# Pooling attention and a four-expert layer: two tiles of the start done alike, with halves and another order

## The chip, the cores and the metric

The kernel runs on one core of one Trainium2 chip. The metric is the time of one execution on the device in microseconds (us), lower being better. A core has five engines that run side by side and wait for one another through semaphores: TensorE multiplies matrices (PE in the profile, and PEld for the loading of its stationary operand), VectorE (DVE) and ScalarE (ACT) work element by element, GpSimd (POOL) here issues nearly all loads, and SyncE (SP) issues the stores and some transposing transfers.

## The reference, cut to what matters

The input is attention with 8 batches, 8 heads, 576 tokens and head size 64. Keys and values are averaged over groups of 8 tokens, so each head has 72 keys. The result goes through four experts whose outputs are added, each weighted by a probability of the token.

```python
k_p = k.reshape(B, H, 72, 8, D).mean(axis=3)          # v_p likewise
scores = scale * q @ k_p.T                            # [576, 72] per head
attn = exp(scores - max(scores)); attn /= attn.sum() + 1e-9
x = (attn @ v_p) as [4608 tokens, 512]
p = domain_probs / (domain_probs.sum(-1) + 1e-9)
out = sum over e of p[:, e] * (relu(x @ w1[e]) @ w2[e])   # w1: 512x1024, w2: 1024x512
```

## The kernel before, in words

A tile is 128 tokens with all 8 heads. There are 36 tiles, and four of them make a group of 512 tokens. A *step* is one group with one expert, and there are 36 steps. In each step `up` (L453) makes the hidden values of 512 tokens, 32 products of 512 columns, and ScalarE applies the relu (L457). `down` (L486) makes the output of one tile, 8 products of 512 columns, and VectorE adds it, weighted, in `collect` (L497, L501). A steady loop at the end of the kernel goes through the steps. While it computes one step's `down` it computes the next step's `up`, and a plan by slots puts the attention of later tiles between them. It starts with `up` of step 1.

Ahead of that loop stands the *head*: the attention of the first four tiles, step 0's `up` for each of them alone (`up_tile`, L469, 32 products of 128 columns), and step 0's `down` of tiles 0 to 2. The head is written out by hand in the order in which each engine is to run it. The kernel has a manual schedule: every engine runs its instructions in the order in which they are written, and a wait holds up everything behind it on that engine.

The attention of a tile goes through these functions, which the change and the prediction name:

- `split_q` and `turn_q` (L310, L314): queries to bf16, turned on TensorE, and copied out of PSUM by ScalarE as `qT`.
- `scores` (L320): products with the keys, into the one PSUM buffer `sc`. The next tile's scores wait until VectorE has read it.
- `maxima` (L334) and `less` (L338), together `less_max`: the greatest score of each head, and the difference from it, on VectorE.
- `expo`: the exponential on ScalarE. For a tile that is "in rows" (`in_rows`) it writes bf16 `attn` undivided (L351). For the others it writes f32 `e_sb` (L358).
- `normalise` (L372 to L380): four VectorE instructions, the sum by head, the small constant, the reciprocal and the division, which writes bf16 `attn`.
- `attn_T` (L394, L395): five transposes on TensorE, and a copy out of PSUM as `attnT`.
- `context` (L436, L442): eight products which give x already turned, and a ScalarE copy to `xT`, the input of `up_tile`.
- `context_rows` (L410, L416), used for tile 0 and for the tiles from the third group on: five products that give x in rows, one token to a partition. VectorE divides by the sum while it copies to `x_sb`.
- For tile 0 alone, `sums0` (L636 to L643) gets the sums by five small products with the 0/1 mask `own`, and `turn_x0` (L648, L649) turns `x_sb` by four transposes and one ScalarE copy.

The values of batch 0 are summed by eight products (`sum_values0`, L615) and spread into `vbd` by two VectorE instructions that multiply by the mask `mask_v` (`spread_values0`, L624). `make_mask_v` (L185) writes that mask from `own`, which GpSimd makes early. `idle_products` (L572) are products of a zeroed tile whose result nobody reads. They stand where TensorE would wait.

PSUM buffers come from pools. `ps_t` (tag "t") and `ps_h` (tag "h") have two buffers each, which alternate, `ps_o` has two, and `ps_s` has one. GpSimd's queue issues the loads in a fixed order: keys and values of batch 0, `w1` of expert 0 in two halves, `w2` of expert 0, `w1` of expert 1, and so on. From the ninth load on each issue waits until the load eight places before it has landed.

Of the kernel before, what the change touches and what calls it, by code (L numbers as in the profile page):

```python
# [10 lines left out]
ALU = mybir.AluOpType  # L11
AX = mybir.AxisListType
BF16 = mybir.dt.bfloat16
F32 = mybir.dt.float32
# [3 lines left out]
def kernel(  # L18
# [10 lines left out]
    nc = tc.nc  # L29

    B, H, S, D = q.shape
    E, DM, F = moe_w1.shape
    P = nc.NUM_PARTITIONS
# [3 lines left out]
    KC = DM // P  # L37
    FB = F // P
    NTOK = B * S
    G = 512  # L40
    NG = NTOK // G
    TPG = G // P
# [7 lines left out]
    V_MEAN = 1.0 / POOL  # L50
# [133 lines left out]
    def make_mask_v():  # L184
        nc.vector.tensor_copy(  # L185
            out=mask_v[:].rearrange("p a z y d -> p (a z y) d"),
            in_=own[:].rearrange("p a z y -> p (a z y)").unsqueeze(2).to_broadcast(
                [P, NPAIR * 4, D]
            ),
        )  # L190
# [97 lines left out]
    attnT = {}  # L288
    xT = {}
# [4 lines left out]
    def by_dma(t):  # L294
        return t >= 2 * TPG


    def in_rows(t):
        return t == 0 or by_dma(t)

    def turn_q(t):
        qT[t] = qtp.tile([P, NPAIR, P], BF16, name="qT")
# [40 lines left out]
    def less_max(t):  # L343
        maxima(t)
        less(t)
# [55 lines left out]

    def context_rows(t):
        ps = ps_t.tile([P, DM], F32, tag="t", name="x_ps")
        for b, _, n, at in segments(t * P, P):
            flat = vbd[b][:].rearrange("p a z y d -> p (a z y d)")
            for i in range(NB):
                c0, c1, h0 = chunk(i)
                nc.tensor.matmul(  # L410
                    ps[at:at + n, h0 * D:(h0 + c1 - c0) * D],
                    lhsT=attnT[t][:, i, at:at + n], rhs=flat[:, c0 * D:c1 * D],
                    start=(i == 0), stop=(i == NB - 1), skip_group_check=True,
                )
        x_sb = soft.tile([P, DM], BF16, name="x_sb")
        nc.vector.scalar_tensor_tensor(  # L416
            out=x_sb[:].rearrange("p (h d) -> p h d", d=D),
            in0=ps[:].rearrange("p (h d) -> p h d", d=D), scalar=V_MEAN,
            in1=rss[t][:].unsqueeze(2).to_broadcast([P, H, D]),
            op0=ALU.mult, op1=ALU.mult,  # L420
        )
        return x_sb

    def context(t):
        g, col = t // TPG, (t % TPG) * P
        if t % TPG == 0:
            xT[g] = grp.tile([P, KC, G], BF16, name="xT")
        if by_dma(t):
            x_sb = x_sbs[t] = context_rows(t)
# [12 lines left out]
        nc.scalar.copy(out=xT[g][:, :, col:col + P], in_=ps[:])  # L442
# [14 lines left out]
        nc.scalar.activation(out=hs[s][:, fb, :], in_=ps[:], func=ACT.Relu)  # L457


    def up_tile(s, i):  # L460
        g, e = divmod(s, E)
        if i == 0:
            hs[s] = hpool.tile([P, FB, G], BF16, name="h_sb")
        cols = slice(i * P, (i + 1) * P)
        for f0 in range(0, FB, TPG):
            ps = ps_h.tile([P, TPG, P], F32, tag="h", name="h_ps")
            for f in range(TPG):
                for kc in range(KC):
                    nc.tensor.matmul(  # L469
                        ps[:, f], lhsT=w1_sb[e][:, kc, (f0 + f) * P:(f0 + f + 1) * P],  # L470
                        rhs=xT[g][:, kc, cols], start=(kc == 0), stop=(kc == KC - 1),
                    )
# [92 lines left out]
    def split_q(c):  # L565
        nc.scalar.copy(out=qrow[c][:], in_=qg[:, :, c, :])


    def idle_products(n):
        ps = ps_o.tile([P, DM], F32, name="o_ps")  # L570
        for _ in range(n):
            nc.tensor.matmul(ps[:], lhsT=still[:, 0:P], rhs=still[:], start=True, stop=True)  # L572
# [55 lines left out]
            )  # L628


    def sums0():
        ps = ps_o.tile([P, H], F32, tag="o_ps", name="es_ps")
        flat = own[:].rearrange("p a z y -> p (a z y)")
        for i in range(NB):
            c0, c1, h0 = chunk(i)
            nc.tensor.matmul(  # L636
                ps[:, h0:h0 + c1 - c0], lhsT=attnT[0][:, i], rhs=flat[:, c0:c1],
                start=(i == 0), stop=(i == NB - 1), skip_group_check=True,
            )
        es = soft.tile([P, H], F32, name="es")  # L640
        nc.vector.tensor_scalar_add(out=es[:], in0=ps[:], scalar1=1e-9)
        rss[0] = soft.tile([P, H], F32, name="rs")
        nc.vector.reciprocal(out=rss[0][:], in_=es[:])  # L643

    def turn_x0(x_sb):
        ps = ps_t.tile([P, KC, P], BF16, tag="t", name="xT_ps")
        for kc in range(KC):
            nc.tensor.transpose(ps[:, kc], x_sb[:, kc * P:(kc + 1) * P], ident[:])  # L648
        nc.scalar.copy(out=xT[0][:, :, 0:P], in_=ps[:])  # L649

    idle_products(14)
    split_q(0)
    split_q(1)
    turn_q(0)
# [3 lines left out]
        turn_keys0(*part)  # L658
        idle_products(2)
    take_keys0()  # L660
    make_mask_v()
    scores(0)
    split_q(2)
    turn_q(2)
    less_max(0)
    split_q(3)
    expo(0)
    idle_products(2)
    spread_values0(sum_values0())
    attn_T(0)  # L670
    scores(1)
    maxima(1)
    idle_products(2)
    sums0()
    turn_q(3)
    idle_products(1)
    xT[0] = grp.tile([P, KC, G], BF16, name="xT")
    x0 = context_rows(0)
    idle_products(4)
    turn_x0(x0)  # L680
    less(1)
    expo(1)
    idle_products(2)
    up_tile(0, 0)
    scores(2)
    normalise(1)
    idle_products(4)
    less_max(2)
    domain_probs0()
    for t in range(1, TPG):  # L690
        attn_T(t)
        if t + 1 < TPG:
            expo(t + 1)
        if t == 1:
            idle_products(3)
        else:
            down(0, t - 1, 0, FB // 2)
        context(t)
        if t == 1:
            scores(3)  # L700
            up_tile(0, t)
            down(0, t - 1)
        else:
            down(0, t - 1, FB // 2, FB)
            up_tile(0, t)
# [56 lines left out]
```

## Time and profile before

| | |
|---|---|
| median of 3 runs | 552.44 us (552.02 to 552.67) |
| the profiled execution's own time | 551.91 us |
| span of the profiled execution, first to last instruction | 549.9 us |
| TensorE busy in the span | 537.4 us (98%) |
| VectorE, ScalarE, GpSimd busy | 264.7, 213.5, 70.7 us |
| first product of the steady loop (L453) | 36.87 us after the span's start |
| TensorE busy in the head, 0 to 36.87 us | 30.85 us |
| TensorE busy in 36.87 to 529 us | 489.50 of 492.13 us |
| transfers in the head, 0 to 36.87 us | 201 GB/s |

The page of the profile cuts the span into 40 slices. The timeline lists instructions in order of time: start, time taken, engine, line, operation, output and input with shapes, how many were merged into the row, and in brackets how long the engine had been idle before and who ended that. The chain of waits follows the work that ended last back through whatever released it. Matmuls overlap, so the time of a merged row is longer than the distance to the next row: five transposes read 0.44 us where the next product starts 0.28 us later.

### The profile page before, as it was taken

What the parts mean: (1) busy time and instruction counts of PE and PEld (TensorE: products, weight loads), DVE (VectorE), ACT (ScalarE), POOL (GpSimd) and SP (SyncE); (2) the same over time, 40 slices, a digit from 0 to 9 for tenths busy, and PEclk for the clock granted to TensorE, in tenths of its full rate; (3) what the DMA queues carried; (4) which work ended last, traced back from release to release, by engine and by line L of the source; (5) the groups of instructions that cost most, each with busy time, mean ns of one, the idle gap of its engine ahead of it and who ended that gap; (6) DMA issues with size and microseconds to landing.
All of it is one profiled execution on the core that took longest, in us unless ns stands there. A gap on an engine that the chain in (4) does not pass through costs nothing.

```text
span 549.9 us, 7267 instructions
## 1 busy us (share of the span) xinstructions
PE 537.4 (98%) x2873; PEld 260.8 (47%) x2929; DVE 264.7 (48%) x456; ACT 213.5 (39%) x355; POOL 70.7 (13%) x120
## 2 busy tenths in 40 slices
PE   7899999999999999999999999999999999999997
PEld 2664554444444444444444444444444444444443
DVE  4874847444744446544554444744473444422223
ACT  3554653333333333333333333333333333333330
POOL 7234001121111100012011100101010000000000
PEclk9999999999999999999999999999999999999999
DMA  9999926556645563367435543335333521111002
GB/s 196 206 202 198 201 19 130 83 67 88 119 72 76 79 121 73 52 83 91 110 54 76 83 108 39 52 42 114 45 54 41 92 57 32 21 39 38 1 1 76
DMA packets 110689, 45.84 MB, mean 83 GB/s; under 512 B 87584, under 2 KB 106016, under 8 KB 110656
## 3 DMA queue, kind: packets, MB, share of 16 engines
q0 software_dynamic: 51472, 22.03, 32.6%
q1 hardware_dynamic: 59184, 23.35, 17.9%
q8 instruction: 23, 0.38, 0.3%
q14 instruction: 10, 0.08, 0.0%
HBM read 45.16 MB, written 9.44 MB: 99 GB/s over the span
## 4 chain that ended last, share of the span: by engine, by line
PE 96%; DMA 1%; DVE 1%; issue 1%; ACT 1%; POOL 0%; POOLq 0%
PE o_ps L486 45%; PE h_ps L453 44%; PE x_ps L410 2%; PE sc L320 2%; PE h_ps L469 1%; DMA kraw<-in_k_dram 1%; PE x_ps L436 1%; PE o_ps L572 0%; PE at_ps L394 0%; ACT attnT L395 0%; PE qT_ps L310 0%; POOL kraw L80 0%; DVE mx L334 0%; DVE d_sb L338 0%; DVE acc L501 0%
## 5 line engine op out<-in xcount | busy, mean ns | idle before, releaser
L457 ACT ACTIVATE h_sb<-h_ps 128x512 bf16<-128x512 f32 x280 | 167.1, 597 | 296.5 <-PE h_ps L453 292.3
L453 PE MATMUL h_ps<-xT,w 128*128 128x512 bf16 x1088 | 271.8, 379 | 1.5
L486 PE MATMUL o_ps<-w,h_sb 128*128 128x512 bf16 x1130 | 270.0, 379 | 1.3
L486 PEld LDWEIGHTS <-h_sb 128*128 128x128 bf16 x1152 | 112.4, 98 | 133.8
L501 DVE SCALAR_TENSOR_TENSOR acc<-o_ps,p_sb,acc 128x512 f32<-128x512 f32 x108 | 81.0, 750 | 180.4 <-PE o_ps L486 177.7
L453 PEld LDWEIGHTS <-w 128*128 128x128 bf16 x1120 | 105.9, 98 | 116.9
L497 DVE TENSOR_SCALAR acc<-o_ps,p_sb 128x512 f32<-128x512 f32 x36 | 27.0, 750 | 60.8 <-PE o_ps L486 60.8
L525 POOL COPY gated<-x_sb 1x1 bf16<-1x1 bf16 x28 | 7.8, 278 | 367.7 <-DVE x_sb L416 367.7
L108 POOL DMA_DIRECT2D qrow<-in_q_dram x36 | 30.5, 850 | 26.3 <-DMA w<-in_moe_w_dram 14.8
L334 DVE TENSOR_REDUCE mx<-sc 128x8 f32<-128x576 f32 x36 | 27.2, 756 | 10.8 <-PE sc L320 10.6
L338 DVE TENSOR_TENSOR d_sb<-sc,mx 128x576 f32<-128x576 f32 x36 | 27.3, 757 | 1.2
L416 DVE SCALAR_TENSOR_TENSOR x_sb<-x_ps,rs 128x512 bf16<-128x512 f32 x29 | 20.1, 692 | 12.5 <-PE x_ps L410 12.1
L351 ACT ACTIVATE attn<-d_sb 128x576 bf16<-128x576 f32 x29 | 19.8, 682 | 3.7 <-DVE d_sb L338 0.5
L372 DVE TENSOR_REDUCE es<-attn 128x8 f32<-128x576 bf16 x28 | 20.8, 744 | 0.0
L410 PEld LDWEIGHTS <-attnT 128*128 128x128 bf16 (+1 forms) x160 | 12.2, 100 | 7.3 <-issue 1.3
L320 PE MATMUL sc<-kT,qT 128*128 128x144 bf16 (+1 forms) x160 | 15.0, 227 | 0.2 <-DVE kT L609 0.2
L320 PEld LDWEIGHTS <-qT 128*128 128x128 bf16 (+1 forms) x160 | 11.1, 100 | 8.4 <-issue 2.2
L410 PE MATMUL x_ps<-vbd,attnT 128*128 128x192 bf16 (+5 forms) x160 | 14.7, 231 | 0.0
L572 PE MATMUL o_ps<-still 128*128 128x512 bf16 x36 | 11.4, 435 | 1.4 <-DVE still L144 1.3
L235 DVE TENSOR_TENSOR vraw<-vraw 128x1280 bf16<-128x1280 bf16 (+1 forms) x14 | 9.2, 654 | 0.2
L235 DVE TENSOR_TENSOR kraw<-kraw 128x1280 bf16<-128x1280 bf16 (+1 forms) x14 | 9.0, 640 | 0.2
L469 PE MATMUL h_ps<-xT,w 128*128 128x128 bf16 x128 | 7.8, 219 | 0.7 <-ACT xT L442 0.4
(76 smaller groups left out, 148.8 us busy)
## 6 DMA issues: line engine op xcount, KB each, us to landing
out_dram<-acc SPq DMA_DIRECT2D x36, 256.0 KB, 2.2
vraw<-in_v_dram POOLq DMA_DIRECT2D x8, 512.0 KB, 6.7
w<-in_moe_w_dram POOLq DMA_DIRECT2D x8, 512.0 KB, 16.1
w<-in_moe_w_dram POOLq DMA_DIRECT2D x4, 1024.0 KB, 16.2
kraw<-in_k_dram POOLq DMA_DIRECT2D x7, 512.0 KB, 6.2
qrow<-in_q_dram POOLq DMA_DIRECT2D x28, 128.0 KB, 4.0
qg<-in_q_dram SPq DMA_DIRECT2D x1, 1024.0 KB, 5.8
kraw<-in_k_dram POOLq DMA_DIRECT2D x2, 256.0 KB, 6.7
```

The lines of the kernel that those rows point to most:

```text
L108: nc.gpsimd.dma_start(out=qrow[t][at:at + n], in_=q[b][:, tok:tok + n, :].rearrange("h p d -> p h d"),)
L320: nc.tensor.matmul(sc[at:at + n, pair // 2, (pair % 2) * PW:(pair % 2 + 1) * PW], lhsT=qT[t][:, pair, at:at + n], rhs=kT[b][:].rearrange(" ...
L334: nc.vector.reduce_max(out=mxs[t][:], in_=by_head(t), axis=AX.X)
L338: nc.vector.tensor_tensor(out=st[t][:], in0=by_head(t), in1=mxs[t][:].unsqueeze(3).to_broadcast([P, 2, 4, SP]), op=ALU.subtract,)
L372: nc.vector.reduce_sum(out=es[:], in_=e, axis=AX.X)
L410: nc.tensor.matmul(ps[at:at + n, h0 * D:(h0 + c1 - c0) * D], lhsT=attnT[t][:, i, at:at + n], rhs=flat[:, c0 * D:c1 * D], start=(i == 0), s ...
L416: nc.vector.scalar_tensor_tensor(out=x_sb[:].rearrange("p (h d) -> p h d", d=D), in0=ps[:].rearrange("p (h d) -> p h d", d=D), scalar=V_ME ...
L453: nc.tensor.matmul(ps[:], lhsT=w1_sb[e][:, kc, fb * P:(fb + 1) * P], rhs=xT[g][:, kc, :], start=(kc == 0), stop=(kc == KC - 1),)
L457: nc.scalar.activation(out=hs[s][:, fb, :], in_=ps[:], func=ACT.Relu)
L486: nc.tensor.matmul(ps[:], lhsT=hs[s][:, fb, i * P:(i + 1) * P], rhs=w2_sb[e][:, fb, :], start=(fb == 0), stop=(fb == FB - 1),)
L497: nc.vector.tensor_scalar_mul(out=accs[t][:], in0=ps[:], scalar1=p_sb[:, e, t:t + 1])
L501: nc.vector.scalar_tensor_tensor(out=accs[t][:], in0=ps[:], scalar=p_sb[:, e, t:t + 1], in1=accs[t][:], op0=ALU.mult, op1=ALU.add,)
```

## The change

Tile 1 joins the tiles that are "in rows". Its exponentials are written undivided as bf16, its sums come from products with `own`, its context is computed in rows, and its x is turned on TensorE. For this `sums0` and `turn_x0` become `sums_by_products(t)` and `turn_x(t, halves)`. For tiles 0 and 1 the division writes x in two halves of four heads each, into two tiles, and the turn takes each half by itself: two transposes and a ScalarE copy for each. The first half's PSUM buffer comes from `ps_t` and the second's from `ps_h`.

`make_mask_v` moves ahead of `split_q(0)`, so on VectorE it stands before the folding of the keys. `scores(1)` moves ahead of `attn_T(0)`. `context_rows(0)` moves ahead of `turn_q(3)`. `up_tile(0, 0)` is split in two with `attn_T(1)` between the parts, and that `attn_T(1)` copies `attnT` on VectorE where it was ScalarE. `scores(2)` stands behind the context of tile 1, and `scores(3)` behind `up_tile(0, 1)`. `down(0, 0)` comes ahead of the loop over tiles, which now runs over tiles 2 and 3, and `collect(0, 0)` comes behind `less_max(3)`. There are 29 idle products where there were 38. The steady loop, the loads and their order are unchanged.

```diff
     def in_rows(t):
-        return t == 0 or by_dma(t)
+        return t < 2 or by_dma(t)
...
-    def context_rows(t):
+    def context_rows(t, parts=1):
         ps = ps_t.tile([P, DM], F32, tag="t", name="x_ps")
...
-        x_sb = soft.tile([P, DM], BF16, name="x_sb")
-        nc.vector.scalar_tensor_tensor(
-            out=x_sb[:].rearrange("p (h d) -> p h d", d=D),
-            in0=ps[:].rearrange("p (h d) -> p h d", d=D), scalar=V_MEAN,
-            in1=rss[t][:].unsqueeze(2).to_broadcast([P, H, D]),
-            op0=ALU.mult, op1=ALU.mult,
-        )
-        return x_sb
+        n = H // parts
+        x = [soft.tile([P, n * D], BF16, name=f"x_sb{i}of{parts}") for i in range(parts)]
+        for i in range(parts):
+            heads = slice(i * n, (i + 1) * n)
+            nc.vector.scalar_tensor_tensor(
+                out=x[i][:].rearrange("p (h d) -> p h d", d=D),
+                in0=ps[:].rearrange("p (h d) -> p h d", d=D)[:, heads], scalar=V_MEAN,
+                in1=rss[t][:, heads].unsqueeze(2).to_broadcast([P, n, D]),
+                op0=ALU.mult, op1=ALU.mult,
+            )
+        return x
...
-    def up_tile(s, i):
+    def up_tile(s, i, starts=tuple(range(0, FB, TPG))):
...
-        for f0 in range(0, FB, TPG):
+        for f0 in starts:
...
-    def sums0():
+    def sums_by_products(t):
...
-    def turn_x0(x_sb):
-        ps = ps_t.tile([P, KC, P], BF16, tag="t", name="xT_ps")
-        for kc in range(KC):
-            nc.tensor.transpose(ps[:, kc], x_sb[:, kc * P:(kc + 1) * P], ident[:])
-        nc.scalar.copy(out=xT[0][:, :, 0:P], in_=ps[:])
+    def turn_x(t, halves):
+        n = KC // 2
+        for i, pool, tag in ((0, ps_t, "t"), (1, ps_h, "h")):
+            ps = pool.tile([P, n, P], BF16, tag=tag, name="xT_ps")
+            for kc in range(n):
+                nc.tensor.transpose(
+                    ps[:, kc], halves[i][:, kc * P:(kc + 1) * P], ident[:]
+                )
+            nc.scalar.copy(
+                out=xT[0][:, i * n:(i + 1) * n, t * P:(t + 1) * P], in_=ps[:]
+            )
+        idle_products(1)
 
     idle_products(14)
+    make_mask_v()
     split_q(0)
...
     take_keys0()
-    make_mask_v()
     scores(0)
     split_q(2)
     turn_q(2)
+    idle_products(2)
     less_max(0)
     split_q(3)
     expo(0)
-    idle_products(2)
     spread_values0(sum_values0())
+    scores(1)
     attn_T(0)
-    scores(1)
     maxima(1)
     idle_products(2)
-    sums0()
+    xT[0] = grp.tile([P, KC, G], BF16, name="xT")
+    sums_by_products(0)
+    x_sb = context_rows(0, 2)
     turn_q(3)
     idle_products(1)
-    xT[0] = grp.tile([P, KC, G], BF16, name="xT")
-    x0 = context_rows(0)
-    idle_products(4)
-    turn_x0(x0)
+    turn_x(0, x_sb)
     less(1)
     expo(1)
+    up_tile(0, 0, (0,))
+    attn_T(1, copy=nc.vector.tensor_copy)
+    up_tile(0, 0, (TPG,))
+    sums_by_products(1)
+    x_sb = context_rows(1, 2)
+    scores(2)
     idle_products(2)
-    up_tile(0, 0)
-    scores(2)
-    normalise(1)
-    idle_products(4)
+    turn_x(1, x_sb)
     less_max(2)
+    expo(2)
     domain_probs0()
-    for t in range(1, TPG):
+    up_tile(0, 1)
+    scores(3)
+    down(0, 0)
+    normalise(2)
+    less_max(3)
+    collect(0, 0)
+    for t in range(2, TPG):
         attn_T(t)
         if t + 1 < TPG:
             expo(t + 1)
-        if t == 1:
-            idle_products(3)
-        else:
-            down(0, t - 1, 0, FB // 2)
+        down(0, t - 1, 0, FB // 2)
         context(t)
-        if t == 1:
-            scores(3)
-            up_tile(0, t)
-            down(0, t - 1)
-        else:
-            down(0, t - 1, FB // 2, FB)
-            up_tile(0, t)
+        down(0, t - 1, FB // 2, FB)
+        up_tile(0, t)
         if t + 1 < TPG:
             normalise(t + 1)
-        if t == 1:
-            less_max(3)
-        if t == TPG - 1:
+        else:
             make_mask_k()
         collect(0, t - 1)
```

More of the change, by code (lines that the diff above doesn't have):

```diff
@@ L428, in context @@
         if by_dma(t):
-            x_sb = x_sbs[t] = context_rows(t)
+            (x_sb,) = context_rows(t)
+            x_sbs[t] = x_sb
             nc.sync.dma_start_transpose(out=xT[g][:, :, col:col + P], in_=x_sb[:])
@@ L457, in up @@
         nc.scalar.activation(out=hs[s][:, fb, :], in_=ps[:], func=ACT.Relu)
-    def up_tile(s, i):
+    def up_tile(s, i, starts=tuple(range(0, FB, TPG))):
         g, e = divmod(s, E)
-        if i == 0:
+        if s not in hs:
             hs[s] = hpool.tile([P, FB, G], BF16, name="h_sb")
         cols = slice(i * P, (i + 1) * P)
-        for f0 in range(0, FB, TPG):
+        for f0 in starts:
             ps = ps_h.tile([P, TPG, P], F32, tag="h", name="h_ps")
@@ L636, in sums0 @@
             nc.tensor.matmul(
-                ps[:, h0:h0 + c1 - c0], lhsT=attnT[0][:, i], rhs=flat[:, c0:c1],
+                ps[:, h0:h0 + c1 - c0], lhsT=attnT[t][:, i], rhs=flat[:, c0:c1],
                 start=(i == 0), stop=(i == NB - 1), skip_group_check=True,
@@ L641, in sums0 @@
         nc.vector.tensor_scalar_add(out=es[:], in0=ps[:], scalar1=1e-9)
-        rss[0] = soft.tile([P, H], F32, name="rs")
-        nc.vector.reciprocal(out=rss[0][:], in_=es[:])
-    def turn_x0(x_sb):
-        ps = ps_t.tile([P, KC, P], BF16, tag="t", name="xT_ps")
-        for kc in range(KC):
-            nc.tensor.transpose(ps[:, kc], x_sb[:, kc * P:(kc + 1) * P], ident[:])
-        nc.scalar.copy(out=xT[0][:, :, 0:P], in_=ps[:])
+        rss[t] = soft.tile([P, H], F32, name="rs")
+        nc.vector.reciprocal(out=rss[t][:], in_=es[:])
+    def turn_x(t, halves):
[10 more added lines that the diff above has]
+        idle_products(1)
     idle_products(14)
+    make_mask_v()
     split_q(0)
```

## The prediction

> **What bounds the kernel now.** First the slices of the page, which say what is busy over the whole span:
>
> ```profile
> PE   7899999999999999999999999999999999999997
> DMA  9999926556645563367435543335333521111002
> ```
>
> TensorE is full but for the first slices, and those are also where the transfers are full. The table of stages says how much lies there:
>
> ```profile
> 0.00:36.87 36.87, 30.85 (x290) 19.22 (x295) 23.69 (x57) 17.39 (x28) 17.07 (x33) 1.00 1.17 201
> 36.87:529.00 492.13, 489.50 (x2511) 233.95 (x2559) 235.04 (x392) 192.57 (x321) 53.63 (x88) 1.00 0.47 76
> ```
>
> The columns are the stage, its length, and the busy time of TensorE, its weight loads, VectorE, ScalarE and GpSimd, then the granted clock. After 36.87 us TensorE is busy 489.50 of 492.13 us with work that the change leaves alone. Before that it waits, or runs idle products. So the change is worth what it moves the first product of the steady loop, now at 36.87. The chain of waits shows what holds the head:
>
> ```profile
> 11.84 0.69 DVE mask_v L185
> ...
> 12.56 0.77 DVE mx L334
> ...
> 15.38 0.70 ACT attnT L395
> ...
> 16.12 0.28 PE es_ps L636 x5
> 16.40 0.24 PE qT_ps L310 x4
> 16.65 0.22 PE o_ps L572
> 16.86 0.33 PE x_ps L410 x5
> 17.20 0.86 PE o_ps L572 x4
> 18.06 0.34 PE xT_ps L648 x4
> ...
> 18.42 0.59 ACT xT L649
> ...
> 19.05 1.95 PE h_ps L469 x32
> ```
>
> The head is one tile's latency after another: a hop from engine to engine, with fillers (L572) beside. The mask's copy stands on the chain. The durations and marks that I use come from the timeline:
>
> ```profile
> 16.44 0.17 DVE L641 TENSOR_SCALAR es<-es_ps 128x8 f32<-128x8 f32 x1
> 17.23 0.69 DVE L416 SCALAR_TENSOR_TENSOR x_sb<-x_ps,rs 128x512 bf16<-128x512 f32 x1 [0.39 <-PE x_ps L410]
> 23.90 0.68 POOL L108 DMA_DIRECT2D qrow<-in_q_dram  x1 [5.09 <-DMA w<-in_moe_w_dram]
> 24.45 1.95 PE L469 MATMUL h_ps<-xT,w 128*128 128x128 bf16 x32 [0.42 <-ACT xT L442]
> 27.97 0.44 PE L394 MATMUL at_ps<-ident,attn 128*128 128x128 bf16 x5
> 30.55 1.95 PE L469 MATMUL h_ps<-xT,w 128*128 128x128 bf16 x32
> 42.74 0.26 ACT L227 COPY p_sb<-pt 128x128 f32<-128x128 f32 x1
> 47.31 0.49 DVE L269 COPY kT<-kT_ps 128x640 bf16<-128x640 bf16 x1 [0.39 <-PE kT_ps L265]
> ```
>
> Start to start on TensorE: `up_tile` 1.79 us (24.45 to 26.24), `down` 1.73 (26.24 to 27.97), five transposes 0.28, four scores 0.24, `context_rows` 0.33, `turn_q` 0.21, a filler 0.22, the five sums 0.15. A wait from one engine to the next costs 0.03 to 0.06. Successive VectorE or ScalarE instructions that need nothing of each other overlap by about 0.06 (x_sb ends at 17.92, the next starts at 17.84).
>
> **Unknown prices.** Half an x_sb (128x256) is in no row. Its bounds are 0.17 us (8 columns) and 0.69 (512). In proportion between them it is 0.43, and 0.36 until the next may start, so two halves end 0.10 after the whole would but the first is ready 0.26 sooner. Half a copy of xT lies between 0.26 (128 columns) and 0.58 (512): 0.37, and 0.31 until the next. I take these, since both rows are the same kind of pass over PSUM. The copy of `attnT` on VectorE is priced by L269, the same shape: 0.49 (ScalarE took 0.69).
>
> **Mask.** `own` is ready at 6.01 and the folding of the keys starts at 7.84, waiting for keys. The 0.69 us copy fits between: cost nothing, with 1.1 us to spare, and a dearer copy would cost only beyond that. Scores(0) end at 12.27, so the maxima start at 12.31 where they started at 12.56: 0.25 won. The exponential then ends at 14.58. It does not move the value sums, which wait for their load until 12.89, so `vbd` is still done at 15.48. Scores(1) run in TensorE's wait (from 13.97, when the scores buffer is read) and no longer stand behind the transposes.
>
> **Tile 0.** Transposes at 14.64, `attnT` copied 15.13 to 15.82, sums at 15.87, context 16.02 to 16.35 with its result at 16.52. VectorE: maxima(1) until 16.18, sum and reciprocal 16.19 to 16.59, x halves done at 17.06 and 17.41. But `turn_q(3)` now runs behind the context (to 16.56), ScalarE copies it 16.76 to 17.34, and the first half's transposes take the PSUM buffer that this copy frees. So a new wait: transposes at 17.39, not 17.12, with only a filler and the second half behind. Copies of x 17.72 to 18.09 and 18.03 to 18.40. `up_tile` does two products after the first copy and goes on at 18.45: as good as a start at 18.34, against 19.05. Won 0.71, of which 0.25 is the mask.
>
> **Tile 1.** Before, 5.40 us lie between the two `up_tile` starts (19.05, 24.45), with scores(3) among them and seven fillers (L572). Now: first half of `up_tile` to 19.23; exp(1) ends at 19.02, so the transposes go at once, to 19.51; VectorE copies until 20.21 while the second half runs to 20.41. Four VectorE instructions of `normalise` (0.75, 0.17, 0.20, 0.76) leave this path, and two small ones (0.17, 0.20) and five sums (0.15) come in. Sums result 20.69, reciprocal done 21.13, halves of x at 21.59 and 21.94, transposes at 21.65 and 22.00, copies to 22.35 and 22.70, `up_tile(0, 1)` as if from 22.64. So 4.30 in place of 5.40; scores(3), 0.24, follow it now. Won 0.86.
>
> **Tiles 2 and 3.** `up_tile(0, 1)` ends at 24.43, scores(3) at 24.67, `down(0, 0)` at 26.40. It needs `w2` of expert 0, landed by 23.90: margin 0.77. VectorE: x(1) 21.94, less_max(2) 23.41, exp(2) 24.12, `domain_probs0` 24.16 hidden beside it, `normalise(2)` (1.99) 26.15. So the transposes of tile 2 start at 26.40 against 27.97: 1.57. Then less_max(3) comes later than before in relation: done at 27.70, exp(3) to 28.42, and the copy of x(2), queued behind it on ScalarE, ends at 28.94. TensorE is free for `up_tile(0, 2)` at 28.98: cover, but only just. `collect(0, 0)` and `normalise(3)` end at 30.45, ahead of their need at 30.78. From there to the steady loop the order is unchanged.
>
> **Sum.** 0.71 + 0.86 = 1.57 us. Nothing is queued differently for GpSimd and SyncE: their instructions stand in the same order, with the same loads. The profiled execution, 551.91 us (span 549.9 and 2.0 around it), would become 550.34; it lies 0.53 under the median of the runs, so the forecast is 552.44 - 1.57 = 550.87 us. With whole prices for halves (0.69, 0.58) tile 0 wins 0.5 less and tile 1 0.73 less: 0.34 in all, 552.10. With halves at the lower ends, at most about 0.5 more: 2.05, 550.39.
>
> **A rule against the change.** GpSimd issues loads at 5.97 to 8.3, just when the mask's copy now runs (6.05 to 6.74). Two issues at 5.97, with VectorE idle, took 1.52 together; others beside VectorE's folding took 0.79 and 0.74. So the row's price is nothing, but no row has this copy beside an issue. The Trainium skill, page "SBUF — State Buffer", section "SBUF: two separate sides", says that a VectorE copy in a two-port mode locks GpSimd out, so that it can't write the descriptors of its transfers. By that rule those issues come up to 0.69 later and `w2` would land at 24.59, still before its need at 24.67: the sum stays, its margin is gone.
>
> **Rivals.**
> 1. VectorE becomes the bound. From 14.2 to 27.7 its rows (spread, maxima, differences, sums, halves, `attnT`, `domain_probs0`, `normalise(2)`) add to 11.4 us, and at `up_tile(0, 2)` TensorE has 0.04 us to spare. Every 0.1 us that halves or small instructions cost more goes through. With half of the difference to the whole prices the gain is 0.95: 551.5; with all of it 552.1. For it: the chain is serial. Against: two rows on either side of each price.
> 2. The weights' landing. If `w2` lands later than 24.67, `down(0, 0)` waits; at 1 us late the gain is 0.8: 551.6. Against: the load's place in the queue is unchanged.
> 3. The steady loop takes the gain back, because it waits for a load that comes no sooner: 552.4. The next needs are `w1` of expert 1 (landed by 28.83) and `w2` of expert 1 (by 42.68, first used 48.20, then about 46.6): covered by 3.9.
> 4. Slower: the clock. The kernel's first fillers start 0.43 us apart until 4.66 and then 0.22: TensorE ran at half rate for 3.4 us. Nine fillers are gone. If the head's sparser work put the clock down at 18 us, each 3.4 us at half rate would cost 1.7; two such stretches give 554.3, and from 3.2 us at half rate the change loses. Against: at 8.20 to 11.08 TensorE is busy 1.59 of 2.88 us and keeps its rate, and the sparsest stretch of the new head, 14.2 to 17.9, holds 2.3 us of product starts.
>
> **How the numbers follow.** Forecast as summed, gain 1.1 to 2.05: 0.73, own range 550.4 to 551.4. Rival 1 beyond that: 0.15. Rival 2: 0.03. Rival 3: 0.04. Rival 4: 0.05. A change under 0.2% (1.1 us) can't be told from none in this kernel, so the first case is faster and rivals 1 to 3 mostly the same: faster 0.74, same 0.20, slower 0.06. The range reaches from 550.1 (lower bound of prices, and 0.3 that medians of such runs wander) to 552.1 (the upper bound): the clock and half of rival 3 stay outside.
>
> **What would show it.** The mask's copy before 7 us; maxima(0) near 12.31; first-half transposes of tile 0 released by ScalarE's qT copy; x halves near 0.43; `up_tile` starting at 18.2, 22.4 and 29.0; the steady loop starting at about 35.3. Wrong would be: TensorE waiting at `down(0, 0)` for a load, at `up_tile(0, 2)` for the copy of x, or products of 512 columns 0.43 apart.

## The result, and the profile after

The changed kernel takes 550.75 us (median of 10 runs, 550.54 to 551.48). The kernel before, run beside it on the same chip, takes 551.97 us (10 runs, 551.71 to 552.67). The ratio is 0.9977, with a 95% interval of 0.9968 to 0.9987. It is faster by 1.22 us, 0.23%. That is just above the 0.2% that the prediction took as the least that can be told from no change, and the interval reaches down to 0.13%. The forecast of 550.9 us was met that closely only by luck: the forecast gain of 1.57 us was not reached, and a base that was too high nearly made up for it.

The two slices of the page that answer to those of before:

```profile
PE   6899999999999999999999999999999999999997
DMA  9999926656545553377436552335333421111002
```

The table of stages, cut where the steady loop now starts, with the columns of before:

```profile
0.00:35.57 35.57, 29.53 (x286) 18.73 (x291) 23.39 (x59) 16.78 (x29) 16.76 (x32) 1.00 1.14 201
35.57:527.70 492.13, 489.50 (x2511) 233.94 (x2559) 235.02 (x392) 192.63 (x321) 54.39 (x89) 1.00 0.48 76
```

The steady loop is the same to the hundredth: 489.50 of 492.13 us in both. The head is 1.30 us shorter (36.87 to 35.57). In this execution the keys landed later, though. VectorE folds the keys (adds rows of a group) in parts as they land, and it began the second part, here called the second fold, at 9.41 us instead of 9.12. First the row of before, then that of after:

```profile
9.12 0.75 DVE L585 TENSOR_TENSOR kraw<-kraw 128x512 bf16<-128x512 bf16 x2 [0.20 <-DMA kraw<-in_k_dram]
...
9.41 0.75 DVE L589 TENSOR_TENSOR kraw<-kraw 128x512 bf16<-128x512 bf16 x2 [0.20 <-DMA kraw<-in_k_dram]
```

The loads of the keys are issued at the same times in both (1.33 to 2.87 us). Over the ten kernels here that make the mask early this fold began at 8.91 to 9.41 us, over the four that make it late at 8.94 to 9.12, so the landing scatters and the runs show no delay by the early copy. Counted from that fold, the steady loop starts after 26.16 us instead of 27.75: 1.59 us won, where 1.57 were summed.

The chain of waits through tile 0 of the changed kernel:

```profile
12.60 0.77 DVE mx L334
...
15.41 0.70 ACT attnT L395
...
16.16 0.28 PE es_ps L640 x5
16.44 0.35 PE x_ps L410 x5
16.80 0.24 PE qT_ps L310 x4
...
17.06 0.59 ACT qT L314
...
17.69 0.29 PE xT_ps L654 x2
...
18.00 0.38 ACT xT L657
...
18.43 0.27 PE h_ps L473 x2
```

The mask's copy is gone from the chain. Between the context (x_ps) and the turn of x (xT_ps) stands the new wait that was forecast, ScalarE's copy of qT. The filler products (o_ps) that stood there before no longer appear.

The timeline of the changed kernel shows the steps one by one (start, time taken, engine, line; in brackets the engine's idle time before and who ended it):

```profile
5.98 1.82 POOL L116 DMA_DIRECT2D w<-in_moe_w_dram  x2
6.06 0.69 DVE L185 COPY mask_v<-own 128x1024 bf16<-128x1024 bf16 x1 [3.96 <-POOL own L153]
...
17.00 0.42 DVE L419 SCALAR_TENSOR_TENSOR x_sb0of<-x_ps,rs 128x256 bf16<-128x256 f32 x1
...
17.69 0.27 PE L654 MATMUL xT_ps<-ident,x_sb0of 128*128 128x128 bf16 x2 [0.46 <-ACT qT L314]
...
18.00 0.65 ACT L657 COPY xT<-xT_ps 128x256 bf16<-128x256 bf16 x2 [0.36 <-PE xT_ps L654]
...
19.96 0.49 DVE L395 COPY attnT<-at_ps 128x640 bf16<-128x640 bf16 x1 [1.54 <-PE at_ps L394]
...
23.41 0.68 POOL L108 DMA_DIRECT2D qrow<-in_q_dram  x1 [4.36 <-DMA w<-in_moe_w_dram]
...
24.94 1.89 PE L490 MATMUL o_ps<-w,h_sb 128*128 128x512 bf16 x8
...
26.53 0.40 PEld L394 LDWEIGHTS <-attn 128*128 128x128 bf16 x5 [0.20 <-DVE attn L380]
...
29.26 1.95 PE L473 MATMUL h_ps<-xT,w 128*128 128x128 bf16 x32
```

So the span shrank by what the sum says. But the profiled execution's own time is 551.05 us for a span of 548.6: 2.4 us lie around the span, where the kernel before had 2.0 (551.91 for 549.9). As a median over all runs, time less span is 1.99 to 2.03 us before, by chip, and 2.38 after (spans are given to 0.1 us). Nearly 0.4 us of the gain is lost where the timeline shows no instruction.

### The profile page after: what moved, and what is told of

Read it like the earlier page. It is cut to its first block, busy times and chain, and to the rows that moved or that the text cites. A ratio compares the mean times of both kernels' runs of the same rounds, so it can differ in the third digit from the quotient of the medians.

```text
span 548.6 us, 7264 instructions
## 1 busy us (share of the span) xinstructions
PE 536.1 (98%) x2870; PEld 260.3 (47%) x2926; DVE 264.4 (48%) x458; ACT 213.0 (39%) x356; POOL 71.2 (13%) x120
## 4 chain that ended last, share of the span: by engine, by line
PE 95%; DMA 1%; DVE 1%; issue 1%; ACT 1%; POOL 0%; DVEq 0%; POOLq 0%
PE o_ps L490 45%; PE h_ps L457 44%; PE x_ps L410 2%; PE sc L320 2%; PE h_ps L473 1%; DMA kraw<-in_k_dram 1%; PE x_ps L440 1%; PE at_ps L394 0%; PE qT_ps L310 0%; ACT attnT L395 0%; ACT xT L657 0%; POOL kraw L80 0%; DVE mx L334 0%; DVE d_sb L338 0%; DVE acc L505 0%
## 5 line engine op out<-in xcount | busy, mean ns | idle before, releaser
L529 POOL COPY gated<-x_sb0of 1x1 bf16<-1x1 bf16 x28 | 7.8, 279 | 365.5 <-DVE x_sb0of L419 365.5
L419 DVE SCALAR_TENSOR_TENSOR x_sb0of<-x_ps,rs 128x512 bf16<-128x512 f32 (+1 forms) x30 | 20.2, 674 | 12.4 <-PE x_ps L410 11.7
L576 PE MATMUL o_ps<-still 128*128 128x512 bf16 x27 | 9.3, 458 | 1.3 <-DVE still L144 1.3
```

## The experiments

"Around" is the median of time less span; for the kernel before it is taken over the 93 runs beside the experiments. "Fold to loop" is the distance from the second fold of the keys to the steady loop in the profile, which takes the scatter of the landing out (27.75 before, 26.16 after). The ratios of the experiments are to a kernel before of 551.90 to 551.94 us, run beside them.

| kernel | median us | ratio to before, 95% | around | fold to loop |
|---|---|---|---|---|
| before | 551.97 | 1 | 2.00 | 27.75 |
| changed | 550.75 | 0.9977 [0.9968, 0.9987] | 2.38 | 26.16 |
| tile0_only | 551.18 | 0.9988 [0.9979, 0.9997] | 1.98 | 26.99 |
| mask_late | 550.94 | 0.9983 [0.9974, 0.9992] | 2.35 | |
| mask_early_only | 551.81 | 0.9999 [0.9990, 1.0008] | 1.98 | |
| undivided | 551.07 | 0.9990 [0.9981, 0.9999] | 2.24 | 26.78 |
| q3_early | 550.64 | 0.9981 [0.9972, 0.9989] | 2.35 | 26.02 |
| before_pad4 | 552.38 | 1.0008 [0.9999, 1.0017] | 2.35 | |
| after_trim3 | 550.16 | 0.9968 [0.9956, 0.9981] | 1.98 | 26.15 |
| before_pad20 | 551.92 | 1.0000 [0.9991, 1.0009] | 2.00 | |
| q3_early_pad16 | 550.26 | 0.9968 [0.9956, 0.9980] | 2.01 | 26.02 |
| no_fillers | 553.35 | 1.0026 [1.0018, 1.0035] | 2.36 | |
| q3_trim3_fill4 | 552.79 | 1.0012 [0.9994, 1.0029] | 1.99 | 26.51 |
| q3_early_trim3 | 550.12 | 0.9966 [0.9954, 0.9978] | 1.99 | 26.04 |

### The parts of the gain

**tile0_only.** The changed kernel up to the turn of tile 0's x; from `less(1)` on, tile 1 goes as before.

```diff
-        return t < 2 or by_dma(t)
+        return t == 0 or by_dma(t)
...
     turn_x(0, x_sb)
     less(1)
     expo(1)
-    up_tile(0, 0, (0,))
-    attn_T(1, copy=nc.vector.tensor_copy)
...
-    scores(2)
     idle_products(2)
-    turn_x(1, x_sb)
+    up_tile(0, 0)
+    scores(2)
+    normalise(1)
+    idle_products(4)
     less_max(2)
...
```

> Everything that the change does up to the turn of x of tile 0; tile 1 and the loop as before. Theory A: the steps of tile 0, 0.71 us faster than before, about 551.25 us, so that 0.86 is left for tile 1. Theory B: the mask's 0.25 is missing, 0.46 faster, about 551.5 us. If the order of tiles 1 to 3 is what wins and tile 0 nothing: 552.0 us.

It took 551.18 us against 551.90: 0.72 us won, and 0.76 by fold to loop, where 0.71 was summed. The step from here to the whole change is 0.83 us by fold to loop (0.86 summed), but only 0.43 us in time. The difference is the time around the span, 1.98 here and 2.38 in the whole change. So the loss came in with the part that does tile 1.

**mask_late.** The changed kernel with `make_mask_v` back where it was.

```diff
     idle_products(14)
-    make_mask_v()
     split_q(0)
...
     take_keys0()
+    make_mask_v()
     scores(0)
```

> The mask's copy put back behind the taking of the keys, all else as changed. Theory A (the sum of steps; the first loads landed 0.27 to 0.29 us later in the changed kernel's profile by chance): maxima(0) wait for the mask again, 0.25 us slower than the changed kernel, about 551.0 us, and the keys' landing has nothing to do with it. Theory B (the early copy, which ran beside a GpSimd issue that took 1.08 us instead of 0.77, also holds the first loads): the loads land 0.29 us sooner, which pays for the 0.25, so about 550.7 us, no slower than the changed kernel; the second folding of the keys starts near 9.12 as before, not near 9.41.

550.94 us against 550.75: 0.19 us for the mask, near the 0.25 forecast, though the intervals of the two ratios overlap. The other theory, that the early copy holds up the keys, has nothing for it: the second fold began at 9.09 us here, inside the 8.91 to 9.41 of the kernels with the early copy. The profiled execution had a stretch of half clock in the head (below), so its later marks are not used.

**mask_early_only.** The kernel before with that one line moved.

```diff
     idle_products(14)
+    make_mask_v()
     split_q(0)
...
     take_keys0()
-    make_mask_v()
     scores(0)
```

> The kernel before with the mask's copy moved early, and nothing else. Theory A: 0.25 us faster than before, about 551.7 us, and the keys land as before or at chance. Theory B: same as before, 552.0 us, the second folding of the keys near 9.41 and the GpSimd issue beside the copy near 1.08 us.

551.81 us against 551.90, not to be told from no change. Four of its 11 executions had a mean granted clock below 0.998, against 3 of 33 of the kernel before beside it. Among the others the medians are 551.64 and 551.88, 0.24 us apart: the size that was summed. By itself this would prove little; with mask_late, and with 0.25 us in the marks (maxima(0) 3.19 us behind the second fold instead of 3.44), it makes 0.2 us likely.

**undivided.** The changed kernel with x of tiles 0 and 1 written and turned whole.

```diff
-    def turn_x(t, halves):
-        n = KC // 2
-        for i, pool, tag in ((0, ps_t, "t"), (1, ps_h, "h")):
...
+    def turn_x(t, x):
+        ps = ps_t.tile([P, KC, P], BF16, tag="t", name="xT_ps")
+        for kc in range(KC):
+            nc.tensor.transpose(ps[:, kc], x[0][:, kc * P:(kc + 1) * P], ident[:])
+        nc.scalar.copy(out=xT[0][:, :, t * P:(t + 1) * P], in_=ps[:])
...
-    x_sb = context_rows(0, 2)
+    x_sb = context_rows(0)
...
-    x_sb = context_rows(1, 2)
+    x_sb = context_rows(1)
```

> The changed kernel with one division and one turn of x for tiles 0 and 1 instead of halves. By the steps: tile 0 loses 0.2 us (its first half waits for ScalarE's copy of the queries anyway) and tile 1 about 0.4: about 0.6 slower than the changed kernel, 551.3 us. Rival: the halves' added instructions eat what they save: 550.8 us.

By fold to loop the halves are worth 0.62 us of the 1.59 (26.78 to 26.16). What the other parts of tile 1's new way are worth one by one was not tried. Its timeline at tile 0:

```profile
17.50 0.40 PE L652 MATMUL xT_ps<-ident,x_sb0of 128*128 128x128 bf16 x4 [0.52 <-DVE x_sb0of L419]
...
17.93 0.59 ACT L653 COPY xT<-xT_ps 128x512 bf16<-128x512 bf16 x1 [0.54 <-PE xT_ps L652]
...
18.57 1.05 PE L473 MATMUL h_ps<-xT,w 128*128 128x128 bf16 x16 [0.46 <-ACT xT L653]
```

The transposes wait for the whole x on VectorE, and `up_tile` for the whole copy of 0.59 us. In time the halves brought 0.32 us: this kernel has less time around the span (2.24), and its keys landed 0.26 us sooner in the profiled execution.

**q3_early.** The new wait on ScalarE's qT copy, taken away by an earlier turn of query column 3.

```diff
     scores(1)
+    turn_q(3)
     attn_T(0)
...
     x_sb = context_rows(0, 2)
-    turn_q(3)
     idle_products(1)
```

> The changed kernel with turn_q(3) ahead of attn_T(0), in TensorE's wait for the exponential, instead of behind the context of tile 0. If the wait for ScalarE's copy of the queries, which the prediction saw, costs what the changed kernel's rows say (first transposes at 17.69, x half ready at 17.42): 0.15 to 0.2 us faster than the changed kernel, about 550.55 us, and the first transposes of x released by VectorE. Rival: the copy of the queries now holds the copy of attnT behind it on ScalarE, and nothing is won, 550.75 us.

The first transposes, which ScalarE's copy of qT released in the changed kernel, are now released by VectorE:

```profile
17.28 0.29 PE L654 MATMUL xT_ps<-ident,x_sb0of 128*128 128x128 bf16 x2 [0.47 <-DVE x_sb0of L419]
```

Fold to loop falls by 0.14 us (26.02), and the median by 0.11, to 550.64 us. The forecast had this wait, at 17.39, and counted its cost.

### The time around the span

The time around the span went with the number of instructions on VectorE, those that only wait included: 566 in the kernel before, 567 in tile0_only, 568 in undivided, 570 in the changed kernel, mask_late and q3_early. (The traces list two fewer in each.) Three experiments change that number alone, and one moves three instructions to ScalarE.

**before_pad4.** The kernel before with four VectorE zeroings that nobody reads, ahead of the folding of the keys, where VectorE waits for the load.

```diff
     nc.vector.memset(kT[0][:], 0.0)
+    pads4 = const.tile([P, 4], F32, name="pads4")
+    for c in range(4):
+        nc.vector.memset(pads4[:, c:c + 1], 0.0)
```

> The kernel before with four more VectorE memsets of one column at its very start, where VectorE then waits 5.7 us for keys. The time around the span is 1.97 us in the kernel before, with 566 VectorE instructions in the program, 1.98 with 567 (tile 0 alone), 2.24 with 568 (undivided) and 2.36 with 570 (the changed kernel). Theory: it goes by the number of VectorE instructions, so here, with 570, it is 2.36, the span stays at 549.85 and the time rises 0.39 to about 552.3 us. Rival: it comes with something else in the new part for tile 1; the time stays at 551.9.

552.38 us, and 2.35 us around the span. Four instructions of no use, beside a wait, cost 0.4 us that no line of the timeline shows.

**after_trim3.** The changed kernel with three zeroings moved to ScalarE, which leaves 567 instructions on VectorE.

```diff
-    nc.vector.memset(vraw[0][TAIL:P, NB - 1, :], 0.0)
+    nc.scalar.copy(out=vraw[0][TAIL:P, NB - 1, :], in_=still[TAIL:P, :])
     for t in attn:
-        nc.vector.memset(t[:, ROWS:NB * P], 0.0)
+        nc.scalar.copy(out=t[:, ROWS:NB * P], in_=still[:, 0:NB * P - ROWS])
```

> The changed kernel with three zeroing memsets of the start done by ScalarE instead of VectorE, which leaves 567 VectorE instructions. Theory of the instruction number: time around the span 1.98, span unchanged at 548.4, time 550.35 us, 0.39 faster than the changed kernel. Rival: 2.36 around the span as in the changed kernel, 550.75 us.

550.16 us, 1.98 us around: what was lost there is back. The other 0.2 us is a shorter span; in the profiled execution the keys landed early (fold at 8.94), and fold to loop is unchanged at 26.15.

**before_pad20.** As before_pad4, with twenty zeroings: 586 instructions.

```diff
     nc.vector.memset(kT[0][:], 0.0)
+    pads20 = const.tile([P, 20], F32, name="pads20")
+    for c in range(20):
+        nc.vector.memset(pads20[:, c:c + 1], 0.0)
```

> The kernel before with twenty VectorE zeroings of one column each behind that of the key block, 586 VectorE instructions in all; nothing is left out of the computation. The time around the span was 1.97 us with 566, 2.24 with 568 and 2.36 with 570. Theory one, it grows with the number: by the same slope (about 0.1 us for each) the time around the span would be 3.5 to 4 us and the time 553.5 us or more. Theory two, the number crosses one border between 567 and 570, behind which it costs one fixed piece: around the span 2.3 to 2.5 us and the time 552.3 to 552.7 us (0.06 us each for the zeroings would lie beside the wait for the keys, inside the span, and cost nothing).

Both theories fell. 551.92 us, 2.00 us around: with twenty instructions more the loss is gone again. The cost neither grows with the number nor stays behind a border. It was seen at 568 and 570; where between 570 and 586 it ends was not measured.

**q3_early_pad16.** q3_early with sixteen such zeroings, 586 instructions again.

```diff
     nc.vector.memset(kT[0][:], 0.0)
+    pads16 = const.tile([P, 16], F32, name="pads16")
+    for c in range(16):
+        nc.vector.memset(pads16[:, c:c + 1], 0.0)
```

> The changed kernel with query column 3 turned earlier (550.64 us, 2.35 us around the span, with 570 VectorE instructions) and sixteen VectorE zeroings of one column each behind that of the key block, which makes 586. In the kernel before, 566 and 586 instructions both gave 2.0 us around the span, and 570 gave 2.35. If the time around the span goes by the number of VectorE instructions alone, not monotonically, and not by what the rest of the program is, sixteen useless instructions more make this kernel faster: around the span 2.0 us, time 550.3 us. If it goes by the change's other edits as well, or by ScalarE's number (the three zeroings that brought 1.98 us were given to ScalarE), around the span stays at 2.35 us and the time at 550.6 to 550.7 us. The zeroings (about 0.06 us each) end before the keys land and should cost the span nothing.

550.26 us against 550.64, and 2.01 us around: sixteen useless instructions made the kernel 0.38 us faster. So the number of VectorE's instructions decides, also in the changed kernel. Why is open. The pages' part on DMA queues shows one difference. First q3_early, with 570 instructions:

```profile
q14 instruction: 10, 0.08, 0.0%
```

Then q3_early_pad16, with 586:

```profile
q14 instruction: 11, 0.09, 0.1%
```

The columns are packets, MB and share of the span. With 586 instructions one more block of about 8 KB of instructions is loaded within the span; the records put it at 540.4 us, 8 us before the end. With 566 to 570 none falls there. This tells 586 from the others, but not 566 from 570. Nor does a load behind the span: in all 14 kernels the records have one, of 8 KB, 1.4 to 1.7 us after the last instruction, whatever the time around. That the end of VectorE's program lies near the border of a block would fit; it is not shown, and what the 0.39 us is made of was not seen.

### The clock

**no_fillers.** The changed kernel without the 15 idle products that run behind the first 14: six in the loop over the keys, two in `turn_x`, seven between.

```diff
     idle_products(14)
...
         turn_keys0(*part)
-        idle_products(2)
...
     turn_q(2)
-    idle_products(2)
...
     maxima(1)
-    idle_products(2)
...
     turn_q(3)
-    idle_products(1)
...
     scores(2)
-    idle_products(2)
     turn_x(1, x_sb)
```

> The changed kernel without any idle product but the first 14 (15 fewer, so sparser yet than the change made it). If the forecast's rival 4 (the clock falls when the head gets sparser) is near: granted clock 0.996 or lower in most executions, TensorE products 0.43 us apart somewhere in the head, and 0.7 to 1.7 us slower, 551.4 to 552.4. If fillers don't matter: 550.75 us or a little less, with clock 0.999 in most executions.

553.35 us: 2.6 us slower than the changed kernel and slower than before. All 11 executions have a mean granted clock of 0.988 to 0.994. The table of stages for TensorE (length, busy time, granted clock, share of transfers, GB/s):

```profile
8.00:12.00 4.00, 1.16 (x8) 0.67 1.22 198
12.00:16.00 4.00, 3.96 (x25) 0.50 1.24 206
16.00:20.00 4.00, 2.25 (x30) 0.93 1.24 207
20.00:24.00 4.00, 3.67 (x42) 0.62 1.25 209
```

The clock is at half for some 7 us and then for about 3 more. So the 15 fillers behind the first 14 hold the clock up. Taking away nine shows no cost: the granted clock is 1.00 in the head of the changed kernel, and the head came out as summed.

The column has a gap: in both kernels the first fillers start 0.43 us apart until 4.66 us and then about 0.22, yet it reads 1.00 there, because its records begin only at 4.7 to 4.9 us.

A fall to half clock happens now and then with all fillers in place, too. In the profiled execution of mask_early_only:

```profile
7.00:9.00 2.00, 1.08 (x10) 1.00 1.23 201
9.00:11.00 2.00, 1.31 (x8) 0.84 1.24 205
11.00:13.00 2.00, 2.00 (x9) 0.50 1.24 203
13.00:15.00 2.00, 2.00 (x16) 0.81 1.24 206
```

TensorE waits for the keys from 7 us on, and its clock is at half for 0.64 + 2.00 + 0.76 = 3.4 us (twice the shortfall from 1.00, by stage length). That execution took 552.78 us against a median of 551.81. The kernel before had a mean clock below 0.998 in 11 of 93 executions and the changed one in 2 of 10, so the change did not bring it.

**q3_trim3_fill4.** The kernel q3_early_trim3 (below) with twice the fillers in that stretch.

```diff
     for part in ((P, 0, 2), (P, 2, 4), (TAIL, 4, 5)):
         fold_keys0(*part)
         turn_keys0(*part)
-        idle_products(2)
+        idle_products(4)
```

> The same kernel with four idle products of 512 columns instead of two behind each of the three parts of the key transposes. Theory: the executions with a mean granted clock of 0.996 to 0.997 (about 1 in 8 over all kernels so far) come from one stretch of 3.41 us in which TensorE had too little to do while it waited for the keys; six more products of about 0.21 us there fill it, no execution is below 0.998, and the median is that of the kernel without them or up to 0.1 us less: 549.9 to 550.2 us. The rival: the fillers stand in front of the next part's transposes and of the scores of tile 0, which then begin 0.4 us later (the last two fillers behind the third part lie on the path), and the time is 550.3 to 550.6 us, with or without the low clock.

Theory and rival both fell short. Three of 12 executions still had a mean clock below 0.998. All three are among the longest (554.39, 554.58 and 555.99 us). Whether their clock fell in the wait for the keys or in a stop of TensorE like the one below can't be told without their traces, so whether these fillers cure it stays open. Fold to loop grew by 0.47 us, as the rival had it, and four executions lie at 550.46 to 550.72 us. But the other eight took 552.47 to 555.99 us, which neither foresaw. One of them, at 553.32, was profiled. Its timeline, SyncE's transposing transfer and TensorE:

```profile
130.56 2.30 SPq L434 DMA_TRANSPOSE xT<-x_sb0of  x1
...
138.16 1.02 PE L457 MATMUL h_ps<-xT,w 128*128 128x512 bf16 x4 [2.38 <-issue]
```

The transposed x took 7.5 us to land (130.56 + 7.5 = 138.06), where 2.5 is the median, and TensorE stood for 2.38 us in a loop that is otherwise full. The profile names nothing that ended this wait, but the products that follow read that x, 0.1 us after it landed. The same transfer in q3_early_trim3:

```profile
129.75 1.19 SPq L434 DMA_TRANSPOSE xT<-x_sb0of  x1
```

What differs is in the DMA view. For q3_trim3_fill4, 131 to 132 us:

```profile
q8 instruction: 1, 0.02, 7.4%
...
xT<-x_sb0of SPq DMA_TRANSPOSE x1, 7.5
```

For q3_early_trim3 no instructions are loaded there; the load comes at 136 to 137 us. In this execution, with six more products ahead of it, a load of instructions fell onto the transfer. That it slowed the transfer rests on the count of such meetings in the last section; the other seven long executions left no trace.

### A version that beats both

**q3_early_trim3.** q3_early and after_trim3 together.

```diff
-    nc.vector.memset(vraw[0][TAIL:P, NB - 1, :], 0.0)
+    nc.scalar.copy(out=vraw[0][TAIL:P, NB - 1, :], in_=still[TAIL:P, :])
...
-        nc.vector.memset(t[:, ROWS:NB * P], 0.0)
+        nc.scalar.copy(out=t[:, ROWS:NB * P], in_=still[:, 0:NB * P - ROWS])
...
     scores(1)
+    turn_q(3)
     attn_T(0)
```

> The changed kernel with both edits that each shortened it: query column 3 turned between the scores of tile 1 and the weight transposes of tile 0 (550.64 us by itself), and the three zeroings of tails on ScalarE instead of VectorE, which leaves 567 VectorE instructions (550.16 us by itself). If the two are of different kinds, as I hold (one shortens the span by 0.14 us, the other the time around the span from 2.36 to 1.98 us), they add: 550.75 - 0.14 - 0.39 = 550.2 us, or 550.0 us if the earlier landings of the keys in the run with the zeroings moved were its doing; around the span 1.98 us. The rival: the zeroings delay ScalarE's query copies by what they take there, the first transposes wait for ScalarE again, and the time is 550.2 to 550.3 us with a steady loop that starts 26.2 us or more behind the second fold of the keys instead of 26.0.

550.12 us (549.99 to 550.44), 0.9966 of before. The first transposes are released by VectorE, fold to loop is 26.04 us and 1.99 us lie around: the two gains add. Against the changed kernel that is 0.63 us, of which 0.11 to 0.14 is the earlier turn and 0.39 the time around the span. The rest, some 0.1 us, goes with early keys (fold at 8.91). Whether the moved zeroings have a part in that is open: the three kernels that have them folded at 8.91, 8.94 and 9.24 us, the other eleven at 8.94 to 9.41.

## Why the prediction was right, and where it was not

**The marks.** With the keys' 0.29 us taken off, each forecast mark came out within 0.05 us:

| step | forecast | measured | less 0.29 |
|---|---|---|---|
| maxima(0) | 12.31 | 12.60 | 12.31 |
| first-half transposes, behind the qT copy | 17.39 | 17.69 | 17.40 |
| `up_tile(0, 0)` goes on behind the second copy | 18.45 | 18.70 | 18.41 |
| `up_tile(0, 1)`, as if from | 22.64 | 22.90 | 22.61 |
| `down(0, 0)` | 24.67 | 24.94 | 24.65 |
| transposes of tile 2 | 26.40 | 26.67 | 26.38 |
| `up_tile(0, 2)` | 28.98 | 29.26 | 28.97 |
| steady loop | 35.30 | 35.57 | 35.28 |

`up_tile(0, 1)` makes two products at 22.69 and goes on at 23.02, so it runs as if from 23.02 less 0.12.

**The mask** ran at 6.06, 0.25 won in the marks, 0.2 in the runs. **Tile 0**: 0.71 forecast, 0.72 to 0.76 in tile0_only. **Tile 1**: 0.86 forecast, 0.83 in the marks.

**The unknown prices** held: half an x took 0.42 us (0.43 forecast), two halves of xT 0.65 in tile 0 (0.68 by 0.31 and 0.37), `attnT` on VectorE 0.49. The range's ends, whole prices on one side and the lower bounds on the other, were not needed.

**Rival 1, VectorE.** It was as tight as written: the weight loads for the transposes of tile 2 waited 0.20 us for VectorE's division, until 26.53. The transposes lost nothing by it, for they began at 26.67, just as `down` was through (24.94 and its 1.73). `up_tile(0, 2)` started at 29.26, when the copy of x had ended at 29.18, and did not wait.

**Rival 2, the landing of `w2`.** GpSimd's next issue waits for it, and went out at 23.41, 1.5 us ahead of `down(0, 0)` at 24.94. The margin scatters with the landings: in q3_early_trim3 that issue went out at 23.98 and `down(0, 0)` began at 24.32, 0.34 us later. **Rival 3** did not come: the steady loop took 492.13 us in both.

**The rule that was weighed.** Before, the two issues at 5.97 us took 1.52 us together; beside the mask's copy they take 1.82, the first of them 1.08 instead of 0.77, in every kernel that makes the mask early. So the direction of the rule (the Trainium skill, "SBUF — State Buffer", section "SBUF: two separate sides") is in the rows, 0.3 us of it and not the 0.69 that it was priced at, and no cost shows: the issue that waits for `w2` went out 14.00 us behind the second fold against 14.78 before, and over all kernels 13.66 to 15.07 us behind it with the early copy and 13.55 to 14.86 without.

**Rival 4, the clock.** The mechanism is real, as no_fillers shows (2.6 us). The argument against it was too strong in one point: that TensorE "keeps its rate" at 8.20 to 11.08 us was true of the execution that was read, and not of every execution of the same kernel.

**What failed** is the last step, the carrying over from the span to the time. The prediction set out from "span 549.9 and 2.0 around it" and took the 2.0 us as staying. They became 2.38: that is the term of the sum that was missing, 0.39 us. Working from the profiled execution, 551.91 - 1.57 = 550.34; add 0.29 for the later keys and 0.39 around the span, and it is 551.02 against 551.05 measured. The forecast time was met all the same, by luck, because its base, the median of three runs, was 0.47 us above the median of ten; from that median the sum gives 550.40, 0.35 us too low. A gain of 1.22 us in place of 1.57 also put the change right at the edge of the 0.2%.

## What to carry to other kernels

Where a full loop follows a latency-bound start, walking the marks hop by hop with prices from neighbouring rows forecasts the start to a few hundredths of a microsecond; take one landing as the origin when two profiles are compared, because landings scatter (here by 0.5 us) by more than some parts are worth. Then compare time less span as well: a kernel can lose there what it won in the span, and adding a few useless instructions on one engine, or taking a few away, shows whether that is so. When products are added or removed far ahead of a long loop, look also at where the loads of instructions fall in that loop; the one long execution traced here points there.

## What the runs showed of the hardware that was not expected

**Time outside the span depends on the length of one engine's program, and not monotonically.** With 566 or 567 VectorE instructions 1.98 to 2.03 us lie around the span, with 568 2.24, with 570 2.35 to 2.38, with 586 2.00 to 2.01, whichever kernel they stand in. What happens in that time stays open.

**Loads of instructions hold up transposing transfers.** Over the 14 profiled executions of this study, 58 of 1,246 transposing transfers behind 30 us kept SyncE's queue for more than 1.5 us instead of 1.2. In 54 of the 58 a load of instructions began between 0.2 us before the transfer's issue and 1.2 us after it; of the transfers issued at the usual pace 55 had such a load. So about half of the transfers that a load meets are slowed, and hardly any other. One transfer of x, issued at 231 to 234 us, shows it best. In the seven kernels in which a load began 0.5 to 0.7 us behind its issue it took 1.98 to 2.48 us and landed after 4.4 to 7.5; in the six with no load from 0.2 us ahead of its issue to 1.2 us behind it (the changed kernel stands between, with one at 1.06), 1.19 and 2.5. These delays were covered: behind 38 us TensorE has one idle time over 0.3 us in the 14 executions, the 2.38 us in q3_trim3_fill4. The Trainium skill, page "Runtime: NRT & Kernel Launch", section "Instruction fetch mechanics", says that instructions are fetched in blocks while the current ones run and that crossing a border is mostly hidden. Here most crossings are hidden, but that one was not.

**The clock can fall with TensorE busy more than half of the time.** In mask_early_only it was busy 1.08 of 2.00 us in the stage before the fall and 1.31 of 2.00 in the stage of the fall, and the clock came back after 3.4 us; most executions of the same kernel show no such fall. The records fit a reason for that. The clock changes only at steps of 3.41 us, and where these lie differs from execution to execution. In the step ahead of the fall TensorE was busy 1.80 us in mask_late (6.77 to 10.18), 1.81 in mask_early_only (6.95 to 10.36) and 1.72 in before_pad4 (6.79 to 10.20), and 1.90 and 1.85 ahead of the two falls in no_fillers. In the ten executions without a fall the sparsest step had 1.83 to 2.22. So the clock fell where a step happened to hold little work; the two ranges overlap, and no run here moves the steps on purpose.
